# A11·B11 of chunk pairs 2 to 9 as seven products of quarters, in the gate-and-up stage of a kernel on one core

## The chip, the cores and the metric

The kernel runs on one core of a Trainium2 chip. The metric is the device time of one execution in microseconds (us). Three runs of the kernel before gave 698.74, 699.64 and 699.85 us, a median of 699.64.

## The reference

```
a = x @ dft_hid_re.T ;  b = x @ dft_hid_im.T          # x: 2048 x 512
y = dft_seq_re @ a - dft_seq_im @ b                    # 2048 x 512
h = silu(x @ w1) * (x @ w3)                            # w1, w3: 512 x 1376
g = sigmoid((x * gate_w).sum(-1, keepdims=True))
out = g * y + (1 - g) * (h @ w2)                       # w2: 1376 x 512
```

The change touches only the product of x with w1 and w3.

## The kernel before, in words

All products are made in float32 by three passes over a split number: `split` (L72, L75) has ScalarE (ACT) write a rounded upper part and VectorE (DVE) the rest, and `mm3` (L80) issues three matmuls of 128x512 on TensorE (PE), upper by upper, upper by lower, lower by upper. The matrix products are Strassen-Winograd schemes, so sums of blocks are made on DVE before they are split, and partial products are added in PSUM.

The program runs in three stretches: the products with the hidden DFT matrices (PSUM name dP) to about 81 us, the **gate-and-up stage** to about 290 us, and the long stage of output blocks (name P, the DFT along the sequence and the product with w2) to the end. The gate-and-up stage handles the 1376 columns in eleven chunks of 128, numbered 0 to 10, one `item` (L419) each. For a chunk the stage's product has w1 and w3 as two halves of a 2x2 block scheme of seven products, named by their operands: F2 and B22 and F1 go on top of A11·B11 in one PSUM pair (name X), F3 and F4 into a second (Z), and A12·B21, the part named Yi and Y, into a third. Each of these is 12 matmuls over two row groups of x.

- `first1(c)` (L351) makes A11·B11 of chunk c: 12 matmuls into X. For an odd chunk DVE adds X to the sums S1 (L355) and ACT takes silu of that.
- `second(i, part)` (L380) makes A12·B21 of the chunks 2i and 2i+1 together, as seven products of quarters (21 matmuls instead of 24), in six parts spread over the odd item before: ACT and DVE bring partial sums from PSUM to SBUF (L388, L389, L394, L395, L399, L400), and `begun` (L358) copies X into Y inside PSUM.
- In an item, u2 and u4 are copies of X and Z made on ACT (L429, L431), to which DVE adds later (L441, L445, L446, L461). Both results are stored to DRAM by GpSimd's queue (POOL, L417), named hsp.
- Weights: `load_w(c)` brings 512 KB for chunk c from SyncE's queue (SP); `prep_wa` splits the half that A11·B11, A12·B21 and F4 use, `prep_wb` the sums that F1, F2, F3 and B22 use. `load_wp`, `sum_wp` (four sums of 128x128) and `prep_wp` (a split of 128x896) do the same for the quarters of A12 of a chunk pair. The quarters of x B21 (BT: T1 to T4) are prepared once, before the stage.

Five hooks h0 to h4 (L973 to L1006) in each item place these loads and splits, and also `work`, which takes from a list the preparation of operands for the long stage: loads r (from DRAM, name ab), splits f0P, f2P, f1P, fl2P and fl1P, and their stores to DRAM by POOL (names fsp and lsp, L516 and L560). These forms have no taker in this stage.

Within one engine instructions run in a fixed order, which a scheduler makes from the program text before it runs; those marked `pinned` stay in the order of the text. All SBUF tiles that matter here come from three rings: f4 with 19 buffers of 4 KB a partition (raw loads, sums, u2, u4, s, forms), zo with 8 (split weights) and op with 28 (operands of x). A new tile takes the buffer of the oldest one that is free by the program's order, and the engine that first writes it waits until the last reader of the old tile is done; when that reader is a store, until the store has landed. PSUM is four pairs: X of even chunks, X of odd chunks, Y, Z.

Three f4 buffers are held through the stage before: bth and btl (T3 and T2 of x B21) and btT4.

Of the kernel before, what the change touches and what calls it, by code (L numbers as in the profile page):

```python
# [8 lines left out]
F32R = mybir.dt.float32r  # L9
# [20 lines left out]
def fnet_swiglu_gate_kernel(  # L30
# [40 lines left out]
    def split(hi, lo, src, pin=False):  # L71
        i = nc.scalar.activation(hi, src, AF.Copy)  # L72
        if pin:
            pinned(i)
        nc.vector.tensor_sub(lo, src, hi.bitcast(F32))  # L75
# [169 lines left out]


    WS, WA, WB, WP, BT, BR = {}, {}, {}, {}, {}, {}

    def load_w(c):
        WS[c] = raw(f"ws{c}")  # L250
        nc.sync.dma_start(WS[c], w13[c])

    def prep_wa(c):
        n = 768 if c == NC - 1 else 512
# [6 lines left out]
        WA[c] = half(h, n // 256), half(l, n // 256)  # L261

    def sum_wb(c):

# [16 lines left out]
    def load_wp(i):
        WP[i] = raw(f"wp{i}")
        nc.sync.dma_start(WP[i][:, :512], wp[i])

    def sum_wp(i):

        w = half(WP[i], 8)
        nc.vector.tensor_add(w[:, 4], w[:, 0], w[:, 3])
        nc.vector.tensor_sub(w[:, 5], w[:, 4], w[:, 1])
        nc.vector.tensor_sub(w[:, 6], w[:, 1], w[:, 0])  # L290
        nc.vector.tensor_sub(w[:, 7], w[:, 2], w[:, 5])

    def prep_wp(i):
        h, l = (o.tile([P, 896], F32R, tag=n, name=f"wp{i}{n}") for o, n in ((zo, "zo"), (f4, "f4")))
        split(h, l, WP[i][:, 128:])
        WP[i] = half(h, 7), half(l, 7)

    def load_bt(g):
        BR[g] = raw(f"bt{g}")
        load_head(BR[g], g)  # L300

    def sum_bt():

        b11, b21, b12, b22 = (half(BR[g])[:, q] for g in range(G) for q in range(2))
# [5 lines left out]
    def prep_bt(k):  # L310
        if k == "T1":

            BT[k] = unit(0, 1)
            split(*BT[k], half(BR[0])[:, 0])
        elif k == "T4":
            t = f4.tile([P, 2, 512], F32R, tag="f4", name="btT4")
            BT[k] = t[:, 0], t[:, 1]
            split(*BT[k], half(BR[0])[:, 1])
        else:
            h, l = (f4.tile([P, 1024], F32R, tag="f4", name=f"bt{v}") for v in "hl")  # L320
            split(h, l, BR[1])
            for q, k in enumerate(("T3", "T2")):
                BT[k] = half(h)[:, q], half(l)[:, q]

    def load_b12():
        BR[2] = raw("b12")
        load_head(BR[2], 1, (0, 0))

    def prep_b12():
        split(*unit(0, 1), BR[2][:, :512])  # L330

    def unit(q, g):
        return tuple(v[:, q] for v in XF[g, "B21"])

    def sub(ps, i, n, z, start):
        w = WP[i]
# [43 lines left out]
    def second(i, part, bank=2):  # L380

        c, d = 2 * i, 2 * i + 1
        if part == 0:
            y = Y["i", i] = pair(bank, f"Yi{i}")
            S1[c], S1[d] = raw(f"s1_{c}"), raw(f"s1_{d}")
            sub(y[:, 0], i, 0, unit(0, 0), True)
            sub(y[:, 1], i, 5, BT["T3"], True)
            nc.scalar.activation(S1[c][:, :512], y[:, 0], AF.Copy)  # L388
            nc.scalar.activation(S1[d][:, 512:], y[:, 1], AF.Copy)  # L389
        elif part == 1:  # L390
            y = Y["i", i]
            sub(y[:, 0], i, 4, BT["T2"], False)
            sub(y[:, 1], i, 2, BT["T4"], False)
            nc.scalar.activation(S1[d][:, :512], y[:, 0], AF.Copy)  # L394
            nc.vector.tensor_add(S1[d][:, :512], S1[d][:, :512], y[:, 1])  # L395
        elif part == 2:
            y = Y["i", i]
            sub(y[:, 0], i, 3, BT["T1"], False)
            nc.scalar.activation(S1[c][:, 512:], y[:, 0], AF.Copy)  # L399
            nc.vector.tensor_add(S1[d][:, 512:], S1[d][:, 512:], y[:, 0])  # L400
        elif part == 3:
            begun(c)
        elif part == 4:
            y = Y[c]
            sub(y[:, 0], i, 1, unit(1, 0), False)
            sub(y[:, 1], i, 6, unit(1, 1), False)
        else:
            nc.vector.tensor_add(S1[c], S1[c], flat(Y[c]))
            silu(c)
            WP.pop(i)  # L410

    def store_h(c, n, t):
        if c >= KEPT:
# [5 lines left out]
    def item(c, hooks):  # L419
        x, wa, wb = X[c], WA[c], WB[c]  # L420

        def part(n):
            if c % 2 and c + 2 < NC:
                second((c + 1) // 2, n)

        z = pair(3, f"Z{c}")
# [4 lines left out]
        pinned(nc.scalar.activation(u4, flat(z), AF.Copy))  # L431
# [7 lines left out]
        hooks[1]()  # L439
        prod(x, wb, 1, "F1", False)  # L440
        nc.vector.tensor_add(u4, u4, flat(x))  # L441
        hooks[2]()
        part(2)
        prod(z, wa, 1, "F4", False)
        nc.vector.tensor_add(u2, u2, flat(z))  # L445
        nc.vector.tensor_mul(u2, u2, S1[c])  # L446
        store_h(c, 0, u2)
        part(3)
# [522 lines left out]
    A0 = [(k, q) for k, _ in CHAIN for q in range(NQS[0])]  # L971
    for c in range(NC):
        def h0(c=c):  # L973
            if c + 2 < NC:
                load_w(c + 2)
            if c % 2 == 0 and c // 2 + 1 < NP:
                load_wp(c // 2 + 1)
            if c == NC - 3:
                load_b12()
# [11 lines left out]
        def h2(c=c):  # L991
            work(1 - c % 2)
# [132 lines left out]
```

## Time and the profile before

| | us |
|---|---|
| median of three runs | 699.64 |
| profiled execution, first to last instruction (span) | 696.6 |
| the profiled execution's own time | 699.6 (3.0 lie around the span) |
| PE busy, x3049 matmuls | 691.7 (99%) |
| DVE busy | 591.7 (85%) |
| ACT busy | 363.3 (52%) |
| first matmul of item 1 | 104.79 |
| of item 3, 5, 7, 9 | 142.20, 179.60, 217.00, 254.40 |

A row of the timeline gives the start, the busy time, the engine, the line, the operation, output and inputs, the tile's shape and, in brackets, the idle time of the engine ahead of it and what ended it. The busy time of one instruction includes its drain; instructions that follow without a wait start at shorter distances, so the cost of one is taken from start to start. The rows of a table by windows give each engine's busy time within a stretch.

### The profile page before, as it was taken

The page shows a single profiled execution, that of the slowest core. Times are in us where ns is not written, and L with a number is a line of the kernel's source. Part 1 is how long each engine was busy: PE and PEld are TensorE (multiplying, and loading weights), DVE is VectorE, ACT ScalarE, POOL GpSimd, SP SyncE. Part 2 cuts the span into 40 slices and gives each one's busy share as a digit, 9 for nine tenths or more (in the row PEclk, how much of TensorE's full clock was granted, in tenths as well). Part 3 has the DMA queues.
Part 4 walks back from the last instruction along what each step waited for, and adds up shares of the span by engine and source line. Part 5 has one row for each costly group of instructions (what it writes and reads, how often), then busy time and mean ns, then how long its engine had stood idle before and what let it go on. Part 6 is the DMA issues. An engine that isn't in the chain of part 4 may idle for free.

```text
span 696.6 us, 8670 instructions
## 1 busy us (share of the span) xinstructions
PE 691.7 (99%) x3049; PEld 571.0 (82%) x3049; DVE 591.7 (85%) x667; ACT 363.3 (52%) x426; POOL 93.2 (13%) x145
## 2 busy tenths in 40 slices
PE   9999999999999999999999999999999999999997
PEld 7888888888888888888888888888888888888886
DVE  6999678697979786769997998979998976999886
ACT  6746355555655454474463466455574445544531
POOL 0012212121212220000000011000100020111110
PEclk9999999999999999999999999999999999999999
DMA  8388937587787879696688869889899678898923
GB/s 305 147 289 317 367 146 269 168 320 268 268 321 271 287 276 396 244 348 212 231 301 329 283 189 263 330 267 361 172 329 411 267 140 282 224 351 240 212 34 89
DMA packets 56620, 183.30 MB, mean 263 GB/s; under 512 B 6076, under 2 KB 6844, under 8 KB 56576
## 3 DMA queue, kind: packets, MB, share of 16 engines
q1 hardware_dynamic: 36032, 111.56, 45.1%
q0 software_dynamic: 20400, 71.06, 32.9%
q8 instruction: 24, 0.39, 0.2%
q14 instruction: 20, 0.16, 0.1%
q10 hardware_dynamic: 144, 0.13, 0.1%
HBM read 123.73 MB, written 58.99 MB: 262 GB/s over the span
## 4 chain that ended last, share of the span: by engine, by line
PE 99%; DMA 0%; ACT 0%; DVE 0%; SPq 0%; DVEq 0%; issue 0%
PE P L82 52%; PE X L82 17%; PE dP L82 10%; PE Z L82 9%; PE Lx L82 5%; PE Yi L82 2%; PE Y L82 1%; PE dP L207 1%; PE last L82 1%; DMA dB<-head 0%; ACT dB21h L132 0%; DVE uP L796 0%; SPq L110 0%; DVEq L1121 0%
## 5 line engine op out<-in xcount | busy, mean ns | idle before, releaser
L72 ACT ACTIVATE zh<-B 128x1024 fp32r<-128x1024 f32 (+1 forms) x134 | 137.3, 1029 | 140.6 <-PE P L82 120.9
L75 DVE TENSOR_TENSOR zl<-B,zh 128x1024 fp32r<-128x1024 f32 (+1 forms) x134 | 156.9, 1180 | 24.6 <-ACT zh L72 18.3
L82 PE MATMUL P<-zh,a0P 128*128 128x512 f32 x280 | 87.5, 389 | 0.0
L82 PE MATMUL P<-zh,f1P 128*128 128x512 f32 x256 | 81.2, 390 | 0.0
L661 DVE TENSOR_TENSOR B<-B,B 128x1024 f32<-128x1024 f32 (+1 forms) x66 | 78.8, 1203 | 0.3
L82 PEld LDWEIGHTS P<-zh,a0P 128*128 128x128 f32 x280 | 52.6, 188 | 11.0
L82 PE MATMUL P<-zh,a2P 128*128 128x512 f32 x192 | 61.3, 389 | 0.0
L82 PEld LDWEIGHTS P<-zh,f1P 128*128 128x128 f32 x256 | 48.0, 188 | 10.2 <-ACT uP L898 0.3
L82 PE MATMUL P<-zh,f2P 128*128 128x512 f32 x176 | 56.2, 389 | 0.0
L82 PE MATMUL P<-zl,a0P 128*128 128x512 f32 x140 | 54.5, 389 | 0.0
L82 PE MATMUL P<-zl,f1P 128*128 128x512 f32 x128 | 49.8, 389 | 0.0
L72 ACT ACTIVATE zh<-LB 128x1024 fp32r<-128x1024 f32 x28 | 29.8, 1063 | 38.2 <-PE P L82 33.2
L82 PEld LDWEIGHTS P<-zh,a2P 128*128 128x128 f32 x192 | 36.0, 188 | 7.5
L75 DVE TENSOR_TENSOR zl<-LB,zh 128x1024 fp32r<-128x1024 f32 x28 | 34.2, 1220 | 8.9 <-ACT zh L72 8.9
L82 PE MATMUL P<-zh,a1P 128*128 128x512 f32 x128 | 40.9, 389 | 0.0
L82 PEld LDWEIGHTS P<-zh,f2P 128*128 128x128 f32 x176 | 33.0, 188 | 6.8
L82 PE MATMUL P<-zl,a2P 128*128 128x512 f32 x96 | 37.3, 389 | 0.0
L82 PE MATMUL P<-zl,f2P 128*128 128x512 f32 x88 | 34.2, 389 | 0.0
L82 PEld LDWEIGHTS P<-zl,a0P 128*128 128x128 f32 x140 | 26.3, 188 | 5.4
L82 PEld LDWEIGHTS P<-zh,a1P 128*128 128x128 f32 x128 | 24.0, 188 | 5.0
L82 PEld LDWEIGHTS P<-zl,f1P 128*128 128x128 f32 x128 | 24.0, 188 | 5.0
L82 PE MATMUL P<-zl,a1P 128*128 128x512 f32 x64 | 24.9, 389 | 0.0
(1077 smaller groups left out, 1550.8 us busy)
## 6 DMA issues: line engine op xcount, KB each, us to landing
B<-cc SPq DMA_DIRECT2D x48, 512.0 KB, 8.0
r<-ab SPq DMA_DIRECT2D x24, 512.0 KB, 5.4
hsp<-u POOLq DMA_DIRECT2D x18, 512.0 KB, 5.3
B<-hsp SPq DMA_DIRECT2D x16, 512.0 KB, 5.7
LB<-cc SPq DMA_DIRECT2D x16, 512.0 KB, 6.2
B<-cc POOLq DMA_DIRECT2D x16, 512.0 KB, 6.7
fsp<-f0P POOLq DMA_DIRECT2D x14, 512.0 KB, 4.7
a0P<-fsp SPq DMA_DIRECT2D x14, 512.0 KB, 8.0
```

What stands on the lines that cost most here:

```text
L72: i = nc.scalar.activation(hi, src, AF.Copy)
L75: nc.vector.tensor_sub(lo, src, hi.bitcast(F32))
L82: nc.tensor.matmul(ps, u, v, start=first and n == 0, stop=last and n == 2, skip_group_check=chain)
L207: tc.keep_in_program_order(nc.tensor.matmul(ps[i // 2][:, i % 2], u[:, 0, sl], v[:, 0], start=start, stop=False, skip_group_check=True))
L661: nc.vector.tensor_add(t, t, RAW[b, o, q])
```

## The change

For the pairs (2,3), (4,5), (6,7) and (8,9), A11·B11 is no longer made by `first1` but by `second1(i, part)`, which runs beside `second(i, part)` in the odd item before the pair. It uses seven quarter products as `second` does. The even chunk's result grows in its PSUM pair X. The odd chunk's part SD grows in an f4 buffer: ACT copies partial sums there (L380, L381, L386; line numbers of the changed kernel), DVE adds to it (L387, L391), SM holds a quarter that ACT puts back into PSUM (L392), and in the even item `seeded` has ACT copy SD into PSUM pair 1 (L402) and DVE add it to S1 (L403).

```
+    def second1(i, part):
+        c, d = 2 * i, 2 * i + 1
+        if part == 0:
+            x = X[c] = pair(0, f"X{c}")
+            SD[d], SM[c] = raw(f"sd{d}"), raw(f"sm{c}", 512)
+            sub(x[:, 1], i, 0, unit(0, 0, 0), True, 0)
+            sub(x[:, 0], i, 5, BT["T3", 0], True, 0)
+            nc.scalar.activation(SM[c], x[:, 1], AF.Copy)
+            nc.scalar.activation(SD[d][:, 512:], x[:, 0], AF.Copy)
+        elif part == 1:
+            x = X[c]
+            sub(x[:, 1], i, 4, BT["T2", 0], False, 0)
+            sub(x[:, 0], i, 2, BT["T4", 0], False, 0)
+            nc.scalar.activation(SD[d][:, :512], x[:, 1], AF.Copy)
+            nc.vector.tensor_add(SD[d][:, :512], SD[d][:, :512], x[:, 0])
+        elif part == 2:
+            x = X[c]
+            sub(x[:, 1], i, 3, BT["T1", 0], False, 0)
+            nc.vector.tensor_add(SD[d][:, 512:], SD[d][:, 512:], x[:, 1])
+            pinned(nc.scalar.activation(x[:, 0], SM[c], AF.Copy))
+        else:
+            x = X[c]
+            sub(x[:, 0], i, 1, unit(1, 0, 0), False, 0)
+            sub(x[:, 1], i, 6, unit(1, 1, 0), False, 0)
+            WP.pop((i, 0))
+
+    def seeded(d):
+        X[d] = pair(1, f"X{d}")
+        pinned(nc.scalar.activation(flat(X[d]), SD[d], AF.Copy))
+        nc.vector.tensor_add(S1[d], S1[d], SD[d])
+        silu(d)
...
         part(0)
         hooks[0]()
-        if c + 1 < NC:
+        part1(0)
+        if c + 1 in (1, NC - 1):
             first1(c + 1)
+        elif c + 1 < NC and not inner:
+            seeded(c + 1)
```

What goes with it: quarters of A11 for each pair (`wr`, four loads of 256 KB, four sums of 128x128 and a split of 128x896, whose both parts lie in zo), and once, in item 0, the quarters of x B11: two loads of 512 KB (bt00, bt01), four sums of 128x512 (L322 to L325) and three splits (bt0h and bt0l, bt0T4, and T1 in place of x B11 itself). bt0h, bt0l and bt0T4 hold three more f4 buffers through the stage. `prep_wa` of a chunk in the middle splits only 256 columns, and two chunks share one zo buffer. Three hooks move: `load_w(c + 2)` from h0 to h2, `prep_wa` from h4 to h1 of the next item.

```
             if c % 2 == 0 and c // 2 + 1 < NP:
                 load_wp(c // 2 + 1)
+                load_wp(c // 2 + 1, 0)
...
         def h1(c=c):
             if c + 1 < NC:
+                if 0 < c < NC - 2:
+                    prep_wa(c + 1)
                 prep_wb(c + 1)
+            if c == 0:
+                sum_bt(0)
...
         def h2(c=c):
+            if 0 < c < NC - 3:
+                load_w(c + 2)
+            if c == 0:
+                prep_bt("T3", 0)
...
                 prep_wp(c // 2 + 1)
+                sum_wp(c // 2 + 1, 0)
+            if c == 0:
+                prep_bt("T4", 0)
...
         def h4(c=c):
-            if c + 2 < NC:
+            if c % 2 == 0 and c // 2 + 1 < NP:
+                prep_wp(c // 2 + 1, 0)
+            if c == NC - 3:
                 prep_wa(c + 2)
+            if c == 0:
+                prep_bt("T1", 0)
             work(2)
```

The order of DVE where item 0 turns into item 1 (s1_1 are the sums of chunk 1, u4_0 the copy of Z of item 0, f0P the forms, wp the quarters). Before:

```order
L355 TENSOR_TENSOR s1_1_759<-s1_1_759,X1_832 128x1024
L75 TENSOR_TENSOR f0P21_827<-r011_628,f0P21_827 128x512
L75 TENSOR_TENSOR f0P51_855<-r011_628,f0P51_855 128x512
L75 TENSOR_TENSOR f0P71_873<-r010_626,f0P71_873 128x512
L441 TENSOR_TENSOR u4_0_796<-u4_0_796,X0_744 128x1024
L78 SCALAR_TENSOR_TENSOR r011_628<-r011_628,r010_626 128x512
L288 TENSOR_TENSOR wp1_825<-wp1_825 128x128
```

After (wp11 are the quarters of A12 of pair 1, wp01 those of A11):

```order
L410 TENSOR_TENSOR s1_1_759<-s1_1_759,X1_838 128x1024
L506 TENSOR_TENSOR u4_0_796<-u4_0_796,X0_744 128x1024
L76 TENSOR_TENSOR f0P21_833<-r011_628,f0P21_833 128x512
L322 TENSOR_TENSOR bt00_825<-bt01_827,bt00_825 128x512
L76 TENSOR_TENSOR f0P51_865<-r011_628,f0P51_865 128x512
L323 TENSOR_TENSOR bt01_827<-bt01_827 128x512
L79 SCALAR_TENSOR_TENSOR r011_628<-r011_628,r010_626 128x512
L324 TENSOR_TENSOR bt01_827<-bt01_827,bt00_825 128x512
L301 TENSOR_TENSOR wp11_829<-wp11_829 128x128
L325 TENSOR_TENSOR bt00_825<-bt00_825,bt01_827 128x512
```

The add to u4_0, which needs the last matmul of F1 of item 0, stood behind three forms and now stands ahead of them; the sums of the quarters of x B11 come between the forms.

The order of ACT a little later, with g1_0 the silu of item 0, u2_1 the copy of X of item 1. Before:

```order
L72 ACTIVATE wp1zo<-wp_825 128x896
L72 ACTIVATE wa_909<-ws_823 128x512
L72 ACTIVATE f0P_912<-r_628 128x512
L72 ACTIVATE f0P_916<-r_903 128x256
L457 ACTIVATE g_0_932<-X_744 128x1024
L429 ACTIVATE u_1_937<-X_832 128x1024
```

After, with the tiles' numbers:

```order
L73 ACTIVATE f0P61_911<-r010_626 128x512
L73 ACTIVATE wp11zoh_919<-wp11_829 128x896
L73 ACTIVATE bt0T4_927<-bt00_825 128x512
L73 ACTIVATE f0P31_936<-r011_628 128x512
L73 ACTIVATE f0P42_940<-r021_917 128x256
L524 ACTIVATE g1_0_956<-X0_744 128x1024
L73 ACTIVATE wp01zoh_930<-wp01_831 128x896
L490 ACTIVATE u2_1_961<-X1_838 128x1024
```

The split of wp01 is new and stands behind two forms and g1_0, and ahead of u2_1.

The order of PE in item 1. Before, behind F2 and F3 and the first quarter products of Yi:

```order
L82 MATMUL Yi_965<-bth,wp1zo 128x512
L82 MATMUL Yi_965<-btl,wp1zo 128x512
L82 MATMUL Yi_965<-bth,wp1f_906 128x512
L82 MATMUL X_983<-x0B11h,wa_909 128x512
L82 MATMUL X_983<-x0B11l,wa_909 128x512
```

After, at the same place:

```order
L83 MATMUL Yi_989<-bt1h,wp11f4l 128x512
L83 MATMUL X_1005<-x0B11h,wp01zoh 128x512
L83 MATMUL X_1005<-x0B11l,wp01zoh 128x512
L83 MATMUL X_838<-x0F1h,wb1h 128x512
L83 MATMUL X_838<-x0F1l,wb1h 128x512
L83 MATMUL X_838<-x0F1h,wb1l 128x512
L83 MATMUL X_838<-x0F1h,wb1h 128x512
L83 MATMUL X_838<-x0F1l,wb1h 128x512
L83 MATMUL X_1005<-x0B11h,wp01zol 128x512
```

Where A11·B11 of chunk 2 took the split weights wa, the 31st matmul of the item now takes wp01zoh and the 38th wp01zol.

More of the change, by code (lines that the diff above doesn't have):

```diff
@@ L253, in prep_wa @@
     def prep_wa(c):
+        if 2 <= c < NC - 1:
+            if c % 2 == 0:
+                t = zo.tile([P, 2, 2, 256], F32R, tag="zo", name=f"wa{c}")
+                WA[c] = t[:, 0], t[:, 1]
+                WA[c + 1] = WA[c]
+            h, l = (v[:, c % 2] for v in WA[c])
+            return split(h, l, WS[c][:, 256:512])
         n = 768 if c == NC - 1 else 512
@@ L261, in prep_wa, with second_wa @@
         WA[c] = half(h, n // 256), half(l, n // 256)
+    def second_wa(c):
+        return c % 2 if 2 <= c < NC - 1 else 1
     def sum_wb(c):
@@ L279, in prep_wb, with load_wp, sum_wp @@
         WB[c] = half(h, 4), half(l, 4)
[L281 to L287, printed above, removed]
+    def load_wp(i, p=1):
+        WP[i, p] = raw(f"wp{p}{i}")
+        nc.sync.dma_start(WP[i, p][:, :512], (wr, wp)[p][i])
+    def sum_wp(i, p=1):
+        w = half(WP[i, p], 8)
         nc.vector.tensor_add(w[:, 4], w[:, 0], w[:, 3])
@@ L291, in sum_wp, with prep_wp, load_bt, sum_bt @@
         nc.vector.tensor_sub(w[:, 7], w[:, 2], w[:, 5])
[L293 to L304, printed above, removed]
+    def prep_wp(i, p=1):
+        h, l = (o.tile([P, 896], F32R, tag=n, name=f"wp{p}{i}{n}{v}")
+                for v, (o, n) in zip("hl", ((zo, "zo"), (f4, "f4") if p else (zo, "zo"))))
+        split(h, l, WP[i, p][:, 128:])
+        WP[i, p] = half(h, 7), half(l, 7)
+    def load_bt(g, p=1):
+        BR[g, p] = raw(f"bt{p}{g}")
+        if p:
+            load_head(BR[g, p], g)
+        else:
+            nc.sync.dma_start(BR[g, p], xt[g, XK.index("B11")])
+    def sum_bt(p=1):
+        b11, b21, b12, b22 = (half(BR[g, p])[:, q] for g in range(G) for q in range(2))
         nc.vector.tensor_sub(b11, b12, b11)
@@ L308, in sum_bt, with prep_bt, load_b12, prep_b12 @@
         nc.vector.tensor_sub(b21, b21, b22)
-    def prep_bt(k):
+    def prep_bt(k, p=1):
         if k == "T1":
-            BT[k] = unit(0, 1)
-            split(*BT[k], half(BR[0])[:, 0])
+            BT[k, p] = unit(0, 1, p)
+            split(*BT[k, p], half(BR[0, p])[:, 0])
         elif k == "T4":
-            t = f4.tile([P, 2, 512], F32R, tag="f4", name="btT4")
-            BT[k] = t[:, 0], t[:, 1]
-            split(*BT[k], half(BR[0])[:, 1])
-        else:
-            h, l = (f4.tile([P, 1024], F32R, tag="f4", name=f"bt{v}") for v in "hl")
-            split(h, l, BR[1])
+            t = f4.tile([P, 2, 512], F32R, tag="f4", name=f"bt{p}T4")
+            BT[k, p] = t[:, 0], t[:, 1]
+            split(*BT[k, p], half(BR[0, p])[:, 1])
+        else:
+            h, l = (f4.tile([P, 1024], F32R, tag="f4", name=f"bt{p}{v}") for v in "hl")
+            split(h, l, BR[1, p])
             for q, k in enumerate(("T3", "T2")):
[L323 to L336, printed above, removed]
+                BT[k, p] = half(h)[:, q], half(l)[:, q]
+    def load_b12(p=1):
+        BR[2, p] = raw(f"b12{p}", 512)
+        if p:
+            load_head(BR[2, p], 1, (0, 0))
+        else:
+            nc.sync.dma_start(BR[2, p], xt[1, XK.index("B11"), :, :512])
+    def prep_b12(p=1):
+        split(*unit(0, 1, p), BR[2, p][:, :512])
+    def unit(q, g, p=1):
+        return tuple(v[:, q] for v in XF[g, QUAD[p]])
+    def sub(ps, i, n, z, start, p=1):
+        w = WP[i, p]
         mm3(ps, w[0][:, n], w[1][:, n], z[0], z[1], start, True, True)
@@ L420, in item, with part1 @@
         x, wa, wb = X[c], WA[c], WB[c]
+        inner = c % 2 and c + 2 < NC
         def part(n):
-            if c % 2 and c + 2 < NC:
+            if inner:
                 second((c + 1) // 2, n)
+        def part1(n):
+            if inner:
+                second1((c + 1) // 2, n)
         z = pair(3, f"Z{c}")
@@ L443, in item @@
         part(2)
-        prod(z, wa, 1, "F4", False)
+        part1(2)
+        prod(z, wa, second_wa(c), "F4", False)
         nc.vector.tensor_add(u2, u2, flat(z))
@@ L973, in h0 @@
         def h0(c=c):
-            if c + 2 < NC:
-                load_w(c + 2)
+            if c == 0:
+                load_w(2)
+                load_bt(0, 0)
+                load_bt(1, 0)
             if c % 2 == 0 and c // 2 + 1 < NP:
                 load_wp(c // 2 + 1)
+                load_wp(c // 2 + 1, 0)
             if c == NC - 3:
-                load_b12()
+                load_w(c + 2)
+                load_b12(0)
             work(1)
@@ L991, in h2 @@
         def h2(c=c):
+            if 0 < c < NC - 3:
+                load_w(c + 2)
+            if c == 0:
+                prep_bt("T3", 0)
+            if c == NC - 3:
+                prep_b12(0)
+                load_b12()
             work(1 - c % 2)
@@ L1088 @@
     wq = w13.reshape(2, 2, 2, P, NC, P).transpose(4, 3, 0, 1, 2, 5)
-    wp = wq[: 2 * NP, :, 0, 1].reshape(NP, 2, P, 2, P).transpose(0, 2, 1, 3, 4).reshape(NP, P, 4, P)
-    wp = wp[:, :, [2, 0, 1, 3]].reshape(NP, P, 4 * P)
+    wr, wp = (
+        wq[: 2 * NP, :, 0, k].reshape(NP, 2, P, 2, P).transpose(0, 2, 1, 3, 4).reshape(NP, P, 4, P)[:, :, [2, 0, 1, 3]]
+        .reshape(NP, P, 4 * P) for k in range(2)
+    )
     w2 = np.zeros((NC * P, D), np.float32)
@@ L1110 @@
         "wp": wp,
+        "wr": wr,
         "w2": w2q,
```

19 lines of the change are left out of this document (13 added, 6 removed).

## The prediction

> **What bounds the kernel now.** First I read the page's busy times, the granted clock, the chain that ended last and the waits of PE.
>
> ```profile
> PE 691.7 (99%) x3049; PEld 571.0 (82%) x3049; DVE 591.7 (85%) x667; ACT 363.3 (52%) x426; POOL 93.2 (13%) x145
> PEclk9999999999999999999999999999999999999999
> PE 99%; DMA 0%; ACT 0%; DVE 0%; SPq 0%; DVEq 0%; issue 0%
> PE wps L916 <- PEq L1115: 0.8, 1, 0.8
> ```
>
> PE sets the time: it is busy 691.7 of the span of 696.6 us, and its only listed wait is 0.8 us at the start. So each matmul less is worth its issue interval, as long as nothing makes PE wait. Next, the windows of the gate-and-up stage: columns are PE, PEld, DVE, ACT and POOL busy with counts, then the clock, DMA share and GB/s. The first row is item 0, each other row a pair of items.
>
> ```profile
> 80.80:104.80 24.00, 24.00 (x107) 19.56 (x106) 14.54 (x24) 13.50 (x19) 2.68 (x5) 1.00 0.55 208
> 104.80:142.20 37.40, 37.40 (x167) 30.97 (x166) 28.32 (x46) 19.06 (x29) 8.08 (x14) 1.00 0.63 214
> 142.20:179.60 37.40, 37.40 (x167) 30.97 (x166) 31.09 (x46) 19.86 (x27) 8.13 (x14) 1.00 0.80 288
> 179.60:217.00 37.40, 37.40 (x167) 30.97 (x166) 31.92 (x48) 22.11 (x31) 8.89 (x15) 1.00 0.82 302
> 217.00:254.40 37.40, 37.40 (x167) 30.97 (x166) 30.48 (x42) 20.64 (x28) 8.34 (x14) 1.00 0.76 272
> ```
>
> PE has no gap in any of them, but DVE is busy 28.3 to 31.9 of 37.4 us: there are 5.5 to 9 us to spare in a pair, and only where its work comes in time. Then the timeline of DVE, ACT, POOL and PE around the start of item 1, which gives the prices.
>
> ```profile
> 96.83 1.22 DVE L355 TENSOR_TENSOR s<-s,X 128x1024 f32<-128x1024 f32 x1 [2.79 <-PE X L82]
> 97.96 1.89 DVE L75 TENSOR_TENSOR f0P<-r,f0P 128x512 fp32r<-128x512 f32 x3
> 99.77 1.22 DVE L441 TENSOR_TENSOR u<-u,X 128x1024 f32<-128x1024 f32 x1
> 101.51 0.28 DVE L288 TENSOR_TENSOR wp<-wp 128x128 f32<-128x128 f32 x1
> 101.71 0.29 DVE L290 TENSOR_TENSOR wp<-wp 128x128 f32<-128x128 f32 x1
> 102.11 0.69 DVE L75 TENSOR_TENSOR f0P<-r,f0P 128x512 fp32r<-128x512 f32 x1
> 102.71 0.29 DVE L291 TENSOR_TENSOR wp<-wp 128x128 f32<-128x128 f32 x1
> 102.92 1.22 DVE L445 TENSOR_TENSOR u<-u,Z 128x1024 f32<-128x1024 f32 x1
> 104.05 1.09 DVE L75 TENSOR_TENSOR wp1f<-wp,wp1zo 128x896 fp32r<-128x896 f32 x1
> 105.05 1.22 DVE L446 TENSOR_TENSOR u<-u,s 128x1024 f32<-128x1024 f32 x1
> 106.79 1.02 DVE L75 TENSOR_TENSOR f0P<-r,f0P 128x512 fp32r<-128x512 f32 x2
> 107.88 1.15 POOL L516 DMA_DIRECT2D fsp<-f0P  x2 [0.44 <-DVE f0P L75]
> 109.20 0.42 DVE L267 TENSOR_TENSOR ws<-ws 128x256 f32<-128x256 f32 x1
> 109.53 0.42 DVE L486 TENSOR_TENSOR r<-r 128x256 f32<-128x256 f32 x1
> 103.04 0.95 ACT L72 ACTIVATE wp1zo<-wp 128x896 fp32r<-128x896 f32 x1 [3.89 <-DVE wp L291]
> 103.89 0.61 ACT L72 ACTIVATE wa<-ws 128x512 fp32r<-128x512 f32 x1
> 104.41 0.93 ACT L72 ACTIVATE f0P<-r 128x512 fp32r<-128x512 f32 x2
> 110.43 1.03 ACT L431 ACTIVATE u<-Z 128x1024 f32<-128x1024 f32 x1 [1.69 <-PE Z L82]
> 111.35 1.05 ACT L72 ACTIVATE wb2h<-ws 128x1024 fp32r<-128x1024 f32 x1
> 99.12 0.39 PE L82 MATMUL X<-x1F1h,wb0l 128*128 128x512 f32 x1
> 104.79 0.39 PE L82 MATMUL X<-x0F2h,wb1h 128*128 128x512 f32 x1
> ```
>
> From start to start DVE takes 1.13 us for 1024 columns (102.92 to 104.05), 1.00 for 896 (104.05 to 105.05), 0.60 for 512 (102.11 to 102.71), 0.34 for 256 (109.20 to 109.53) and 0.20 for 128. ACT takes 0.93 for 1024 (110.43 to 111.35), 0.85 for 896, 0.52 for 512, and I take 0.30 for 256. A matmul takes 37.40/165 = 0.2267 (a pair has 165 in the program's order; the windows count those that overlap an edge too). Last, the transfers, in us from issue to landing:
>
> ```profile
> fsp<-f0P POOLq DMA_DIRECT2D x14, 512.0 KB, 4.7
> fsp<-f2P POOLq DMA_DIRECT2D x12, 512.0 KB, 5.0
> r<-ab SPq DMA_DIRECT2D x24, 512.0 KB, 5.4
> lsp<-fl2P POOLq DMA_DIRECT2D x7, 512.0 KB, 6.8
> fsp<-f0P POOLq DMA_DIRECT2D x7, 256.0 KB, 2.8
> ```
>
> **The change part by part.** The profiled execution took 696.6 + 3.0 = 699.6 us, which is the median of the three runs (699.64); I reckon from that.
>
> *What it removes.* Four pairs with 21 matmuls in place of 24: 12 x 0.2267 = 2.72 us, a pair then taking 162 x 0.2267 = 36.72. All of it is on PE, thus on the path.
>
> *DVE, each pair.* Four sums of 128 (0.80), the split of wp0 (1.00) and two adds of 512 (L387, L391: 1.20), less two splits of 512 that become 256 (0.52): +2.5. The add of 1024 to S1 is only exchanged (L355 for L403). With 28.3 to 31.9 busy that goes into a period of 36.7 on average, so by the sum alone it would be hidden.
>
> *ACT, each pair.* The split of wp0 (0.85), copies SM and SD (3 x 0.52), the two copies into PSUM (0.52 and 0.93), less 0.44: +3.4 on 19 to 22. Hidden by the sum. But two of these stand between PE's own matmuls: X is overwritten only after SM and SD are copied.
>
> *Once, in item 0.* Four sums of 512 (2.40), splits of 1024, 512 and 512 (2.33): +4.7 on DVE, beside the first pair's 1.8 for wp01. This has a due time, and here DVE's order decides. L506 now stands directly behind L410, which can end at 97.96, and waits for the last matmul of F1: 99.12 plus its 0.39, and some handing over, 99.57. Before, three forms filled that hole. From 99.57: L506 1.13, then the rows to the last sum of wp01 (L304) are 10 of 512, 8 of 128, 3 of 1024 and 1 of 896: 6.00 + 1.60 + 3.39 + 1.00 = 11.99, so 112.7. ACT's split of wp01 ends at 113.6 at the earliest. PE wants it as the 31st matmul of item 1: 104.79 + 30 x 0.2267 = 111.6. That is 2.0 us. The lower part wp01zol comes 3.7 us of rows later (two of 512, one each of 256, 1024 and 896): 116.4, wanted at 111.6 + 2.0 + 7 x 0.2267 = 115.2, another 1.2. So **DVE alone makes a stall of 3.2 us**, already more than the 2.72.
>
> *Buffers, first pair.* Three more f4 buffers are held, and SD, SM and raw wp0 go through the same ring: 19 less 6 instead of less 3 turn over. A writer now waits for stores to land, in ACT's fixed order. f0P31 waits for f0P71's store: DVE ends f0P71 at 107.2, POOL issues 0.4 later (DVE's first of the two splits ends at 107.48, POOL's issue is 107.88), landing 4.7 later: 112.35. Then g1_0 waits for f0P61's store: DVE 109.2, +0.4 + 4.7 = 114.3. Behind it stand g1_0 (to 115.3), wp01zoh (116.2) and u2_1 (117.1). PE: Yi waits 0.9 for wp11zoh (its last sum comes at 107.4, the split ends at 108.4, wanted at 107.5), X of pair 1 waits from 112.5 to 116.2 = 3.7, F1 for u2_1 0.5, and the copy L392, behind splits that wait for ws3, 1.3. Sum **6.4**: item 3 starts at 142.2 - 0.7 + 6.4 = 147.9.
> A 512 KB store at 4.7 is the price in that. The Trainium skill ("DMA: Bandwidth & Descriptors", Anatomy of one DMA — SWDGE (gpsimd) path) fits 2.0 us plus bytes/436e3, an estimate of 3.2 us here; by it X's wait would be 2.1 in place of 3.7. The row with 4.7 is this kernel's own and I keep it.
>
> *Second pair.* load_w moved from h0 to h2, so ws5 arrives late; wa4, which reads it, stands ahead of g1_3 and u2_4 on ACT, and PE waits 0.95 for u2_4 in item 4, 0.85 in item 3: **1.8**, item 5 at 186.4.
>
> *Third pair.* The load r100 on SP waits for the store of f2P11 to land: u4_4 is copied at 177.3 to 178.3, f2P11 split by 179.5, landed at 179.5 + 0.4 + 5.0, the load 5.4 later: 190.3. ACT's f1P10 waits for it, ahead of g1_4, u2_5 and wp03zoh (0.52 + 0.93 + 0.93 + 0.85), ready at 193.6; PE wants it at 186.4 + 6.8 = 193.2, so 0.4, or 2.8 if the buffer of f2P71's store comes in as late as my count has it. The same with r101 ahead of SM and SD: 1.6, and smaller ones 3.2. Between 5.2 and 7.6; I take **5.2**, since it needs the fewest late landings.
>
> *Fourth pair.* On ACT s1_9 waits for fl2P4's store and SM for fl2P1's, at 6.8 each: **3.2** by the same count.
>
> Sum: 699.64 - 2.72 + 6.4 + 1.8 + 5.2 + 3.2 = **713.5**. The moved prep_wa and the two tiles in zo add nothing: their readers come 10 us later. The bounds: with stores at 2.8, the 256 KB row, the waits behind them are 1.9 shorter each, and what is left is the first pair's 3.2 to 4; with 6.8 they are 2.1 longer in each of four pairs, 722. Below nothing no unknown goes, since PE can't take matmuls faster than it does.
>
> **The rivals.**
>
> 1. *First pair only.* The order runs late once, in item 1, and from there slack returns: while PE waits, stores land and DVE catches up; it has 36.7 - (31.9 + 2.5) = 2.3 us or more in each later pair. For it: the sums. Against: the waits of pairs 3 and 4 are for landings, not for busy engines. Time: 699.64 - 2.72 + 4 to 6.4 = 700.9 to 703.3.
> 2. *All hidden, faster.* Wp01's splits come in time and PE takes 12 matmuls less: 699.64 - 2.72 = 696.9. It decides at one point: wp01zoh by 111.6. For it: DVE would have to be 2.0 us ahead of my rows, as when L506 doesn't wait where I have it. Against: no row shows DVE shorter than start to start. With a stall that only balances the gain (2.7, the DVE figure 3.2 nearly does) it is 699 to 701, no change.
> 3. *The clock drops behind the waits.* The granted clock is 1.00 everywhere here, also behind the only wait of 0.8. Should matmuls run at half rate for about as long as PE waited, each wait would cost half of itself more: 713.5 + 16.6/2 = 721.8. Nothing before shows it. The Trainium skill ("TensorE: Matmul & The Clock Gate", HAM oscillation — how this bites in real kernels) puts the limit at idle gaps over about 3.4 us; no run here shows such a gap yet, and of mine only X's 3.7 would reach it.
>
> That the change doesn't do what it says is no rival: in the program's order each of the four pairs has its three matmuls less.
>
> **How the numbers follow.** A measurement of this kernel tells about 0.2%, 1.4 us. Waits in all pairs (713.5): 0.62. First pair only: 0.20. Hidden: 0.07. Balanced: 0.05. Clock: 0.06. The likeliest alone ranges from 705 (the main wait for a store in each pair 1.9 shorter, which is 7.6) to 721; for eight in ten the range must take in the first rival, so 701 to 721. Faster 0.07, same 0.05, slower 0.62 + 0.20 + 0.06 = 0.88.
>
> **What would show it.** Right: PE waits in item 1 at X of pair 1 for wp01zoh, released by ACT; item 3 starts near 147.9, items 5, 7 and 9 near 186, 228 and 268 in place of 179.6, 217.0 and 254.4; g1_0 on ACT starts past 113; POOL's landings are what ACT's idle time ends on; the span behind the stage is unchanged. Wrong: PE stays at 99% with 3037 matmuls, or item 3 late and items 5 to 9 keeping that distance (first rival), or a granted clock below 1.00.

## The result and the profile after

The changed kernel takes 715.58 us, the median of four runs (714.60 to 717.17), against 699.26 for the kernel before on the same chip: a ratio of 1.0237, 95% interval 1.0222 to 1.0253, so 16.3 us slower. The profiled execution is the slowest of the four, 717.17 with a span of 715.4 (1.8 lie around it), at a mean granted clock of 0.991 where the other three have 0.995.

The page of the changed kernel, with the rows that answer to those shown of before:

```profile
PE 696.9 (97%) x3037; PEld 570.7 (80%) x3037; DVE 607.9 (85%) x703; ACT 379.6 (53%) x454; POOL 93.0 (13%) x145
PEclk9999998999999999999999999999999999999999
```

PE has its twelve matmuls less (3037 against 3049) and is busy longer, in part through the slower clock that the seventh slice shows. The gate-and-up stage now shows holes. Its windows, one pair of items in each row, columns as before:

```profile
105.20:149.80 44.60, 40.24 (x164) 32.17 (x164) 36.43 (x63) 25.70 (x38) 8.72 (x15) 0.92 0.57 198
149.80:188.80 39.00, 37.67 (x163) 30.05 (x162) 33.23 (x50) 23.48 (x34) 8.53 (x15) 1.00 0.73 262
188.80:231.50 42.70, 39.31 (x163) 31.30 (x163) 35.37 (x56) 24.70 (x34) 7.79 (x13) 0.96 0.74 255
231.50:271.10 39.60, 37.79 (x163) 30.02 (x162) 32.51 (x48) 25.77 (x38) 8.85 (x15) 1.00 0.79 290
```

Against the 36.72 us that 162 matmuls take, the pairs lose 7.9, 2.3, 6.0 and 2.9 us, 19.0 together, where 16.6 was predicted. Less the 2.72 saved, and with 0.4 more ahead of item 1 and about 2 behind item 9 (the difference of the time left from there), that is the 18.8 by which the span grew.

The costliest wait, on ACT and PE in item 1 (all rows of ACT in that stretch):

```profile
111.95 0.63 ACT L73 ACTIVATE f0P<-r 128x512 fp32r<-128x512 f32 x1 [0.36 <-DMA fsp<-f0P]
113.72 0.42 ACT L73 ACTIVATE f0P<-r 128x256 fp32r<-128x256 f32 x1 [1.14 <-DMA r<-w]
114.94 1.02 ACT L524 ACTIVATE g<-X 128x1024 f32<-128x1024 f32 x1 [0.80 <-DMA fsp<-f0P]
115.86 0.94 ACT L73 ACTIVATE wp01zoh<-wp 128x896 fp32r<-128x896 f32 x1
116.70 1.02 ACT L490 ACTIVATE u<-X 128x1024 f32<-128x1024 f32 x1
```

```profile
109.09 0.50 PE L83 MATMUL Yi<-x0B21h,wp11zoh 128*128 128x512 f32 x1 [0.97 <-ACT wp11zoh L73]
116.86 0.79 PE L83 MATMUL X<-x0B11h,wp01zoh 128*128 128x512 f32 x1 [3.39 <-ACT wp01zoh L73]
117.45 0.63 PE L83 MATMUL X<-x0B11l,wp01zoh 128*128 128x512 f32 x1
117.88 0.69 PE L83 MATMUL X<-x0F1h,wb1h 128*128 128x512 f32 x1
```

The silu g, ready to go, has no input to wait for but a buffer: what ends its idle time is a store's landing. Behind it on ACT stands the split that PE needs. PE idles 3.39 us, and then matmuls start 0.43 apart in place of 0.23. The windows around that gap show why:

```profile
114.00:116.00 2.00, 0.00 (x0) 0.00 (x0) 0.88 (x2) 1.20 (x3) 1.01 (x2) 1.00 0.65 266
116.00:118.00 2.00, 1.14 (x3) 0.73 (x4) 2.00 (x2) 2.00 (x3) 0.42 (x2) 0.51 0.92 358
118.00:120.00 2.00, 2.00 (x6) 1.59 (x6) 1.04 (x4) 2.00 (x5) 0.39 (x1) 0.50 0.64 244
...
124.00:126.00 2.00, 2.00 (x11) 1.65 (x10) 1.36 (x3) 1.30 (x4) 0.00 (x0) 1.00 0.81 256
```

The granted clock, the column behind POOL's count, is 0.50 after the gap, and 1.00 again from 124 on: fourteen matmuls follow the one before them some 0.2 us later than at full clock.

The other pairs' waits, in the order of the stage:

```profile
PE Yi L83 <- ACT s L444: 1.3, 1, 1.3
PE X L83 <- ACT wp03zoh L73: 0.7, 1, 0.7
PE X L83 <- DVE wp03zol L76: 2.2, 1, 2.2
PE X L83 <- ACT u L490: 0.5, 1, 0.5
PE X L83 <- ACT wp04zoh L73: 0.6, 1, 0.6
PE X L83 <- DVE wp04zol L76: 0.5, 1, 0.5
PE Yi L83 <- ACT s L444: 0.6, 1, 0.6
PE P L83 <- ACT uP L965: 1.7, 1, 1.7
```

The first is pair 2 (item 3), the next three pair 3, then three of pair 4, and the last lies in the long stage.

### The profile page after: what moved, and what is told of

It reads as the page before. It is cut to its first block, busy times and chain, and to the rows that moved or that the text cites. A ratio compares the mean times of both kernels' runs of the same rounds, so it can differ in the third digit from the quotient of the medians.

```text
span 715.4 us, 8729 instructions
## 1 busy us (share of the span) xinstructions
PE 696.9 (97%) x3037; PEld 570.7 (80%) x3037; DVE 607.9 (85%) x703; ACT 379.6 (53%) x454; POOL 93.0 (13%) x145
## 4 chain that ended last, share of the span: by engine, by line
PE 66%; issue 19%; DMA 5%; DVE 4%; POOL 4%; ACT 2%; POOLq 0%; SPq 0%; DVEq 0%; ACTq 0%
PE P L83 46%; PE X L83 5%; PE dP L83 5%; PE Lx L83 5%; PE Z L83 3%; POOL fsp L583 2%; DMA fsp<-f1P 2%; DVE zl L76 2%; DMA r<-ab 1%; PE dP L208 1%; POOL hsp L472 1%; PE last L83 1%; POOL ab L187 1%; DMA fsp<-f0P 1%; PE Y L83 1%
```

## The experiments

My theory was that of the prediction: writers in the f4 ring wait for stores to land, in the fixed order of ACT and DVE, since more of the ring is taken. The rivals: the added work itself in the order of DVE and ACT (a backlog); the moved loads; and the clock. The table gives the length of the four pairs, from the first matmul of items 1, 3, 5, 7 and 9 in the profile of each (36.7 is PE alone with seven products, 37.4 without). The lengths are those of one execution, the time is a median.

| kernel | pair 1 | 2 | 3 | 4 | time, us | ratio to before (95%) |
|---|---|---|---|---|---|---|
| before | 37.4 | 37.4 | 37.4 | 37.4 | 699.26 | |
| changed | 44.6 | 39.0 | 42.7 | 39.6 | 715.58 | 1.0237 (1.0222 to 1.0253) |
| e1 before, 16 buffers | 37.4 | 38.0 | 38.5 | 41.3 | 726.77 | 1.0369 (1.0319 to 1.0419) |
| e2 before + quarters | 39.8 | 37.4 | 37.4 | 37.4 | 702.12 | 1.0038 (1.0025 to 1.0051) |
| e3 changed, no stores | 39.7 | 36.9 | 37.1 | 37.0 | 700.84 | 1.0026 (1.0016 to 1.0037) |
| e5 load_w in h0 | 42.1 | 40.8 | 39.3 | 41.9 | 716.26 | 1.0246 (1.0229 to 1.0263) |
| e7 SM apart | 43.6 | 40.2 | 42.5 | 39.6 | 715.86 | 1.0239 (1.0216 to 1.0262) |
| e9 forms spread | 41.8 | 41.8 | 39.0 | 38.5 | 714.83 | 1.0217 (1.0200 to 1.0233) |
| e10 spread more | 37.0 | 37.8 | 41.5 | 42.7 | 713.70 | 1.0203 (1.0176 to 1.0229) |
| e11 gap filled | 44.1 | 38.4 | 42.9 | 41.0 | 716.98 | 1.0250 (1.0226 to 1.0274) |

### e1 and e2: the three buffers, without and with the work that fills them

e1:

```
-    f4 = ctx.enter_context(tc.tile_pool(name="f4", bufs=19, side="right"))
+    f4 = ctx.enter_context(tc.tile_pool(name="f4", bufs=16, side="right"))
```

> The kernel before with an f4 ring of 16 buffers in place of 19, and nothing else: the three that the changed kernel holds for the quarters of x B11, without its work. Buffer theory (writers wait for stores to land since fewer buffers turn over): PE waits in the gate-and-up stage in several pairs, 703 to 712 us. Rival (the loss is the added work in the fixed order of DVE and ACT): no change, 698 to 701.

e2, added to the kernel before, in item 0:

```
+            if c == 0:
+                for g in range(G):
+                    BR["x", g] = raw(f"bt0{g}")
+                    nc.sync.dma_start(BR["x", g], xt[g, XK.index("B11")])
...
+                split(HELD[0], HELD[1], BR["x", 1])
...
+                split(HELD[2][:, :512], HELD[2][:, 512:], half(BR["x", 0])[:, 1])
...
```

> The kernel before plus the one-time part alone: two loads of 512 KB, four sums of 512 and the splits T3 and T4 in item 0, the three buffers held up to item 8; no product uses them, and T1 is left out. Buffer theory: about as e1, 703 to 712, with the first pair's share larger. Rival of DVE and ACT work: 4.1 us more on DVE once, without wp01, which gives at most 1 to 2 us, and pairs 2 to 4 without a wait.

e1 came to 726.77 us, over the range, but not for the reason that I put it to: its span grew by 30.5 us, of which 5.6 lie in the four pairs and 22.6 behind item 9, in the long stage, where the ring is short as well:

```profile
PE P L82 <- ACT uP L898: 7.4, 4, 4.0
PE P L82 <- DVE zl L75: 4.6, 2, 4.2
PE Yi L82 <- DVE s L395: 2.0, 1, 2.0
```

So it shows that 19 buffers are no spare size; it doesn't measure the change, which takes three away in one stage alone. e2 does that: 702.12, below the 703 of my range. Pair 1 loses 2.4 us and pairs 2 to 4 nothing, with the three buffers held through them. Its waits in the stage, and the windows of pairs 1 and 2:

```profile
PE X L82 <- ACT g L457: 1.1, 1, 1.1
PE Z L82 <- DVE u L445: 0.4, 1, 0.4
```

```profile
105.30:145.10 39.80, 38.31 (x167) 30.67 (x166) 33.98 (x58) 23.48 (x35) 9.16 (x16) 1.00 0.69 241
145.10:182.50 37.40, 37.40 (x167) 30.97 (x166) 31.08 (x46) 19.86 (x27) 8.13 (x14) 1.00 0.80 288
```

Holding buffers is not enough, then, to make pairs 2 to 4 wait. That half of my theory fell, and the pattern is the rival's. Added to the kernel before, without the rest of the change, the one-time part costs 2.4 us in pair 1, where the whole change loses 7.9.

### e3: the changed kernel without the forms' stores

```
-                nc.gpsimd.dma_start(fsp[m, PRODS.index(k), q, :, : 2 * n], flat(t.bitcast(F32)))
+                if (m, k, q) == (0, IN_PLACE[0], 0):
+                    nc.gpsimd.dma_start(fsp[0, 0, 0], flat(t.bitcast(F32)))
...
-            nc.gpsimd.dma_start(lsp[m - 1, PRODS.index(k)], flat(t.bitcast(F32)))
...
```

The long stage reads the one store that stays in place of all, so only the time of this kernel counts.

> The changed kernel without the stores of the forms f0P, f2P, f1P, fl2P, fl1P (one of them stays; the long stage reads that one again in place of all). Their buffers come free when DVE has split, without a landing. Buffer theory: what stays is DVE's backlog in item 1, some 3 us, and the stage ends 10 to 13 us earlier than in the changed kernel: 702 to 706. Rival of DVE and ACT work: 712 to 716.

700.84 us, 15 less than the changed kernel. Pairs 2 to 4 run within 0.4 us of PE alone, though DVE and ACT have the same work in them:

```profile
104.80:144.50 39.70, 37.63 (x164) 30.21 (x163) 36.00 (x63) 25.86 (x39) 3.32 (x5) 1.00 0.38 132
144.50:181.40 36.90, 36.90 (x164) 30.30 (x163) 33.59 (x51) 22.71 (x34) 3.00 (x5) 1.00 0.47 172
181.40:218.50 37.10, 37.10 (x163) 30.17 (x162) 34.39 (x56) 25.12 (x35) 2.87 (x4) 1.00 0.47 156
218.50:255.50 37.00, 37.00 (x164) 30.27 (x163) 32.23 (x48) 25.78 (x38) 2.87 (x4) 1.00 0.47 159
```

DVE is busy 33.6 to 34.4 of about 37 us in pairs 2 and 3, and nothing waits for it. So the rival of the added work is out for pairs 2 to 4: without the stores it is hidden. What stays is 3.0 us in pair 1, where the prediction had 3.2 for DVE's rows alone, and it is more than the 2.72 saved: even without the stores the kernel is not faster than before. Removing the stores takes two things away: landings that buffers wait for, and DMA traffic (the DMA share, the last column but one, falls from 0.73 to 0.47 in pair 2, and a load r of 512 KB in the four pairs takes 3.6 us in place of 5.0). It also lets the scheduler put a few instructions elsewhere (in pair 1 DVE's wp01zol stands ahead of L528, in the changed kernel behind it). How much of the effect is which isn't told apart here; the rows of ACT above, which end on landings, speak for the first.

### e5, e6 and e7: moved loads, an earlier start, one tile less

e5 puts `load_w(c + 2)` back into h0. e6 makes the quarters of x B11 ahead of item 0:

```
+    load_bt(0, 0)
+    load_bt(1, 0)
+    sum_bt(0)
     first1(0)
+    prep_bt("T3", 0)
+    prep_bt("T4", 0)
...
```

and takes the same calls out of the hooks of item 0.

e7 takes SM out of the ring:

```
-            SD[d], SM[c] = raw(f"sd{d}"), raw(f"sm{c}", 512)
+            SD[d], SM[c] = raw(f"sd{d}"), const.tile([P, 512], F32, tag="sm", name=f"sm{c}")
```

> The changed kernel with load_w(c + 2) back in hook h0, where it was before, in all items. If the late arrival of ws is what PE waits for in the second pair (the prediction's step), that pair loses its 2.4 us: 712.5 to 714. Buffer theory: a raw buffer is held some 10 us longer in each item, and waits for landings grow: 716 to 720.

> The changed kernel with the one-time part (loads, sums, T3 and T4 of x B11) ahead of item 0; T1 stays. DVE has 4.1 us less to do in item 0. If DVE's backlog makes the first pair's stall, it falls from 7.9 to under 4 (with the clock's drop gone), 710 to 712, and the rest stays. If waits for landings make it, the three buffers are only held earlier: 714 to 717.

> The changed kernel with SM in a buffer of its own (2 KB, outside the f4 ring), so the ring loses one short-lived tile in each pair. Buffer theory: 1 to 3 us less, 712.5 to 714.5, mostly in the pairs where SM's copy waited. Rival: no change, 715 to 716.

e5: 716.26, no gain; the four losses sum to 17.2 in place of 19.0 (one execution each), and lie elsewhere (pairs 2 and 4 have more, pairs 1 and 3 less). The moved load is not the cause, and the step of the prediction that put the second pair down to it is wrong. e7: 715.86, no change: one tile of the ring in each pair is not worth what I gave it. e6: 720.20 (ratio 1.0294, 1.0266 to 1.0322): slower than the changed kernel, where either view had less or the same. Its waits:

```profile
PE Yi L83 <- ACT s L444: 4.2, 3, 2.3
...
PE X L83 <- ACT wp01zoh L73: 2.1, 1, 2.1
```

X's wait in pair 1 is 2.1 in place of 3.4, and a new wait of 2.3 for the copy L444 comes ahead of item 1, where the buffers are now held. In e6's profile the granted clock is 0.95 from the start, so its pair lengths aren't in the table, and item 1 begins at 111.87 in place of 105.24: PE asks later, and the smaller wait doesn't show by itself that DVE's backlog is less. The median shows that the earlier start gains nothing; that it moved the cost forward is likely and not shown.

### e9, e10 and e12: fewer forms beside the seven products

`work(1)`, `work(1 - c % 2)` and `work(2)` in the hooks become `work(PLAN[c][h])`. The kernel changed has 6 and 4 calls in even and odd items; all forms are done by item 8.

```
e9:   items 0 to 8: 5 and 3 calls;  item 9: 5, item 10: 6
e10:  item 0: 2, items 1 to 8: 3 and 5;  item 9: 7, item 10: 6
e12:  items 0 to 3: 2, 3, 5, 3;  items 4 to 8: 6 each;  item 9: 4
      and second1 for pairs 1 and 2 only (LAST1 = 6):
...
-        if c + 1 in (1, NC - 1):
+        if c + 1 == 1 or LAST1 <= c + 1 < NC:
             first1(c + 1)
...
```

> The changed kernel with the forms spread over eleven items in place of nine: in items 0 to 8 one call less of work in hook h4, the rest in items 9 and 10. Same work, same stores, fewer of their buffers in the ring at a time while the four pairs run. Buffer theory: waits fall in all four pairs, 704 to 711. Rival (the added work of DVE and ACT in its order, or the moved loads): no more than 2 us less, 713.5 to 716.

> As e9_after_spread, with three forms less in item 0 besides (they come in items 9 and 10), where the quarters of x B11 are made. Buffer theory and DVE's backlog in item 1 agree: the first pair's stall falls most; 701 to 708, and below e9_after_spread. Rival (moved loads or the copies into PSUM make the waits): 713.5 to 716.

> The changed kernel with seven products for A11·B11 of pairs 1 and 2 alone (chunks 2 to 5), chunks 6 to 9 by first1 as before with x B11 restored in item 4, so that the three buffers come free there; forms as in e10_after_spread_more in items 0 to 3, six in each of items 4 to 8, the rest in item 9. Six matmuls less than before, 1.36 us. Buffer theory: pairs 1 and 2 wait 1.4 us together as in e10, pairs 3 and 4 nothing: 698.5 to 701. Rival (it is the forms that come late, not seven products beside them, that made pairs 3 and 4 of e10 wait 10.8 us): 704 to 711.

In time e9 (714.83) and e10 (713.70) missed what I expected of them: neither differs clearly from the changed kernel, and both lie in the rival's range. But the place of the loss moved. The windows of e10:

```profile
105.70:142.70 37.00, 37.00 (x163) 30.22 (x162) 33.86 (x53) 23.76 (x35) 7.29 (x12) 1.00 0.56 200
142.70:180.50 37.80, 37.36 (x164) 30.26 (x163) 28.94 (x46) 21.40 (x30) 6.74 (x11) 1.00 0.57 198
180.50:222.00 41.50, 37.77 (x163) 30.08 (x162) 33.32 (x52) 22.56 (x31) 7.26 (x12) 1.00 0.63 219
222.00:264.70 42.70, 39.10 (x163) 31.34 (x162) 31.39 (x47) 25.84 (x37) 7.27 (x12) 0.96 0.69 252
```

Pair 1 runs at 37.0, within 0.3 us of PE alone, with the one-time part, wp01 and three held buffers all in place, and only fewer forms beside them. So the moved loads and the copies into PSUM, e10's rival, don't make pair 1 wait by themselves. Fewer forms are fewer stores and also less work for DVE and ACT; in pair 1 the two aren't told apart. Pairs 3 and 4 now lose 4.8 and 6.0, though they too have fewer forms than in the changed kernel (8 stores of forms in each, in place of 9 and 11); their waits are

```profile
PE X L83 <- ACT X L392: 4.5, 2, 2.9
PE Yi L83 <- ACT s L444: 2.0, 1, 2.0
```

two for the copy of SM back into PSUM, which stands in ACT's order. So the count of forms alone doesn't give the loss; which form falls behind which copy in the order counts too, and this differs from plan to plan.

e12 came to 701.26, slower than before (ratio 1.0026, 1.0010 to 1.0042), 0.3 above the 698.5 to 701 that the buffer theory had, and below its rival's 704. Where it uses seven products, it gains (windows of pairs 1 and 2, then all the waits of the stage):

```profile
105.10:142.20 37.10, 37.10 (x164) 30.26 (x163) 34.06 (x53) 23.90 (x35) 7.31 (x12) 1.00 0.56 199
142.20:179.20 37.00, 37.00 (x163) 30.25 (x162) 27.58 (x44) 21.79 (x31) 6.23 (x10) 1.00 0.58 202
```

```profile
PE Y L83 <- ACT Y L417: 1.5, 1, 1.5
PE X L83 <- DVE u L507: 0.7, 1, 0.7
```

74.1 us for two pairs in place of 74.8: of the 1.36 us of matmuls saved, half comes out as time there. Both waits lie in pair 4. Pairs 3 and 4 have the forms that pairs 1 and 2 gave up (13 and 11 stores), take 77.6 in place of 74.8, and give back more than was gained. No version that I ran is faster than the kernel before.

### e4, e8 and e11: PE kept busy through the gap

Fourteen matmuls by a zero weight are added into Yi of pair 1, so that PE does not idle ahead of X:

```
+            if i == 1:
+                for _ in range(14):
+                    pinned(nc.tensor.matmul(y[:, 1], ZERO, unit(0, 0)[0], start=False, stop=False,
+                                            skip_group_check=True))
...
```

This is their place in e11. To hold it, the first matmuls of X of pair 1 and of F1 are pinned as well (in e8 that of F4 too), so the order of PE in item 1 is not the changed kernel's.

> The changed kernel with 14 matmuls by a zero weight added into Yi of pair 1, right ahead of the first matmul that waits for wp01zoh, so that PE works (14 x 0.2267 = 3.2 us) while it would wait 3.4. If the clock's drop behind that wait costs the 2.8 us that the trace shows (14 matmuls at 0.43 in place of 0.23), it is gone: 712 to 713.5. If the time there is the waits' alone, nothing changes: 715 to 716.

> As e4_after_warm, but with the first matmul of F1 and of F4 of item 1 kept behind the 14 added ones, so that these fill the gap and no other matmul waits in it. PE's gap ahead of X falls under 1 us and the clock stays at 1.00 in item 1. If the drop costs 2.8 us there: 712 to 714, unless the moved order of ACT makes a new wait. If the clock drops all the same: 715 to 717.

> As e8_after_warm_2, with the 14 matmuls by zero ahead of ACT's copies of Yi, so that these wait for them and not the other way round. PE's gap ahead of X falls under 1 us, the clock stays at 1.00 in item 1. If the drop costs 2.8 us there: 712 to 714. If it drops all the same or costs nothing: 715 to 717.

The first two say nothing on the clock. In e4 (722.52, ratio 1.0337, 1.0295 to 1.0379) a matmul of F4 slipped ahead of the added ones and waited 5.1 us; in e8 (721.52, ratio 1.0318, 1.0303 to 1.0333) the added ones had to wait 6.0 for ACT to read Yi first. In both the gap only lay elsewhere. e11, with the fourteen ahead of ACT's copies, fills it. Two of its windows (the clock is 1.00 in all of item 1), and its waits in pair 1, besides the 1.0 for wp11zoh:

```profile
116.00:118.00 2.00, 1.71 (x8) 1.04 (x6) 2.00 (x2) 2.00 (x3) 1.03 (x3) 1.00 0.67 262
118.00:120.00 2.00, 1.45 (x6) 1.24 (x7) 1.04 (x4) 2.00 (x6) 0.26 (x1) 1.00 0.90 336
```

```profile
PE X L83 <- ACT X L396: 1.3, 1, 1.3
PE Z L83 <- ACT u L500: 0.8, 1, 0.8
```

With the gap filled, there is no drop. Yet pair 1 takes 44.1 us against 44.6, and the kernel 716.98. At full clock PE runs into ACT's queue again. The 0.8 is partly the new order: the first matmul of F4, which waits for u4, started at 127.99 in the changed kernel, behind F1, and starts at 118.55 here, ahead of it. The 1.3 is at the very copy (L392 in the changed kernel, L396 here) that the prediction had and the changed kernel doesn't show. Ahead of that copy stands a split f0P that waits for a store to land, first in e11, then in the changed kernel:

```profile
128.41 0.42 ACT L73 ACTIVATE f0P<-r 128x256 fp32r<-128x256 f32 x1 [3.92 <-DMA fsp<-f0P]
128.68 0.42 ACT L73 ACTIVATE f0P<-r 128x256 fp32r<-128x256 f32 x1 [0.57 <-DMA fsp<-f0P]
```

ACT comes to it earlier in e11 and gets past it at nearly the same time. (That store took 4.5 us in e11 and 2.3 in the changed kernel, so the near equality has some luck in it.) Taking the drop away gains no time here; what the drop costs by itself, with the order and the landings unchanged, isn't shown.

## Why the prediction was right, step by step

- **Sign, size and mechanism.** 713.5 was forecast, 715.58 measured. The likeliest case is the one that came: PE waits in all four pairs, and engines that were off the path set the time. That the sum is so near owes something to luck: in pairs 2 and 4 the waits were not the ones named, and the 705 of the range's working should read 705.9.
- **The gain.** 12 x 0.2267 us exists: PE has 3037 matmuls, and e3 and e12 run pairs at 36.9 to 37.1 us.
- **DVE in item 1.** 3.2 us from its rows alone; e3, where stores hold nothing up, leaves 3.0 in pair 1. The total fits better than its parts: the 2.0 at X came as 0.97 for wp11zoh and 0.91 for wp01zoh, one behind the other, and in place of the 1.2 for wp01zol there is only 0.18 for u2_1 (from start to start the three cost PE 2.8).
- **The chain of the first pair.** Item 1 began 0.4 later than in the trace of before. With that, g1_0 was forecast at 114.7 and began at 114.94, on the landing that was named; wp01zoh ended at 116.8 as forecast (116.6). The waits 0.9 and 3.7 measured 0.97 and 3.39. The two small ones behind (0.5 and 1.3) did not come; about 2.8 us of half clock came in their place (14 matmuls about 0.2 later each), so the pair lost 7.9 and not 6.4. e11, which has no drop there, has a wait of 1.3 at L392's copy in its place.
- **A store's price.** The row of 4.7 us for f0P's store was kept against the estimate of 3.2 from "DMA: Bandwidth & Descriptors" (Anatomy of one DMA — SWDGE (gpsimd) path) in the Trainium skill. By that estimate X would have waited 2.1; it waited 3.39, nearer to the row's 3.7. The store that g1_0 waited for, issued at 110.19, took 4.7 us to land, the one before it 3.6. The price goes with the load: the stores hsp of 512 KB in the four pairs take 4.7 in the changed kernel and 3.2, the estimate, in e3.
- **Second pair.** 1.8 forecast, 2.3 measured, and the step was wrong: I put it down to ws5 arriving late. There is such a wait on ACT, but PE's is 1.3 for the copy L444, and e5, with the load moved back, gains nothing. In its place ACT's rows show two splits f2P, at 150.66 and 154.23, that waited 2.59 for a load r and 2.41 for DVE's L551, and from 154.23 to that copy at 159.11 ACT had no gap: ACT's order ahead of the copy, then, which was not tried by itself.
- **Third and fourth pair.** 5.2 and 3.2 forecast, 6.0 and 2.9 measured. Item 5 began 2.4 later than forecast (188.8 for 186.4). With that, f1P's split was due at 192.7 at the earliest and began at 193.12, on the landing of an f2P store, the buffer of my later case; the wait for wp03zoh, 0.4 forecast, measured 0.67. But the larger wait is on wp03zol (2.2), which I didn't have: ACT and DVE stand in the rows

```profile
193.12 0.63 ACT L73 ACTIVATE f1P<-r 128x512 fp32r<-128x512 f32 x1 [1.03 <-DMA fsp<-f2P]
196.37 0.69 DVE L551 TENSOR_TENSOR r<-r,r 128x512 f32<-128x512 f32 x1 [2.54 <-DMA r<-ab]
198.72 1.08 DVE L76 TENSOR_TENSOR wp03zol<-wp,wp03zoh 128x896 fp32r<-128x896 f32 x1
```

  with DVE waiting 2.54 for a load r, ahead of wp03zol. That load is the second of the two that the prediction had behind stores: SP waited 2.7 us for a store of f2P to land, issued it at 190.66, and it took 5.6. The late load was foreseen, the tile that it holds up was not (SM and SD were named). Some 1.5 us more are the clock again. In the fourth pair the size came and the step was wrong: neither s1_9 nor SM waits for a store of fl2P. ACT's idle time that ends on a landing is ahead of wp04zoh, for a store of f1P:

```profile
234.52 1.67 ACT L73 ACTIVATE fl2P<-rl 128x512 fp32r<-128x512 f32 x3 [3.60 <-DMA fsp<-f1P]
```

  PE's waits there are 0.6 and 0.5 for wp04zoh and wp04zol and 0.6 for L444.
- **The clock.** It was given 0.06 as a rival on top of the waits. It happened, in two places, and not as priced: with the gap of pair 1 filled, e11 is no faster. The rule from "TensorE: Matmul & The Clock Gate" (HAM oscillation — how this bites in real kernels) in the Trainium skill, gaps over about 3.4 us, fits the 3.39 of pair 1, but the other gaps don't follow it. In pair 3 the clock fell to 0.72 over six microseconds behind two gaps of 0.67 and 2.19 us, 3.4 us apart. Single gaps of 1.99 (e1), 2.07 (e9) and 2.89 us (e10) were followed by 0.50 too, and gaps of 2.34 (e9), 2.48 (e7) and 2.75 (e5) by 1.00. So gaps well under 3.4 us can be enough here, and the length of a gap alone doesn't tell.
- **Where the reason was too simple.** "Three more buffers held" is only a part (e2: nothing in pairs 2 to 4). The loss needs the stores (e3), the forms beside the seven products (e10 and e12, pairs 1 and 2), and an order in which ACT and DVE have what PE needs behind what waits for a landing. The span behind the stage, forecast as unchanged, grew by about 2 us, 1.7 of it one wait for uP. This wait is 0.9 in e2, e3 and e9 and isn't listed in e5, e7 and e10, which have the change too, so it isn't a fixed part of its cost; where it comes from was not tried.
- **What stays open.** How much is the landing of the stores and how much the traffic that they make for the loads (both show: idle time of ACT and SP that ends on a landing in pairs 1, 3 and 4, and loads r at 5.0 us in place of e3's 3.6), and which of the two kinds of wait a better order could avoid; orders made by hand were not tried.

## What to carry to other kernels

Fewer matmuls are worth their time only where the engines beside PE can deliver in order and in time: here 12 matmuls less cost 16 us, since new copies and splits stand in queues behind instructions that wait for a buffer, and the buffer for a store. Before such a change, don't go by busy times alone (DVE's 34 of 37 us were hidden in e3); follow the order of the queue from one due time of PE backwards, and put landings, not busy times, on the tiles that a DMA reads last. And read a dropped clock as a consequence first: fill the gap, and see whether the time moves (here 716.98 for 715.58).

## What the runs showed of the hardware that was not expected

After PE had idled 3.39 us, the granted clock was 0.50 for about six microseconds, 14 matmuls at 0.43 us, and then 1.00 again; after 3.30 us in e7 it was 0.57 for four. Shorter gaps went both ways: 1.99 (e1), 2.07 (e9) and 2.89 us (e10) were followed by 0.50, and 2.34 (e9), 2.48 (e7) and 2.75 us (e5) by 1.00. With the gap filled by matmuls by zero the clock stayed at 1.00 in item 1 of e11.

Stores of 512 KB on POOL's queue, the same ones (hsp), took 4.7 us at a DMA share of 0.57 to 0.79 in the four pairs of the changed kernel, and 3.2 at 0.38 to 0.47 in those of e3.
